# A hand-written instruction order laid out anew: a fused attention and token-mixing kernel

## The chip, the cores and the metric

The kernel runs on one core of a Trainium2 chip. The metric is the device time of one execution in microseconds; the time before is the median of three executions. A core has five engines that run side by side, each through its own list of instructions in order: TensorE (PE; its weight loads are shown as PEld), VectorE (DVE), ScalarE (ACT), GpSimd (POOL) and SyncE (SP). They wait for one another by semaphores. SP, ACT and POOL also issue DMAs, which run on 16 shared DMA engines.

## The reference

For each of 8 batches, 8 heads, 576 rows `q`, `k`, `v` of 64 and 32 packing rows `p` (all float32):

```python
p_packed = sm_attn(p, k, v)                # 32 rows attend to 576
out      = sm_attn(q, p_packed, p_packed)  # 576 rows attend to the 32 results
x = out.transpose(0, 2, 1, 3).reshape(B, S, H * D)      # [8, 576, 512]
wq, wk = x @ w_q, x @ w_k                               # [8, 576, 64] each
W_tok  = scale * einsum('bsd,btd->bst', wq, wk)
mixed  = einsum('bst,btd->bsd', W_tok, x)
result = maximum(mixed, 0) @ w_out                      # [8, 576, 512] float32
```

`sm_attn` is softmax attention with a scale of 1/8.

## The kernel before, in words

There is no scheduler. A string `ORDER` (lines 13 to 57) names every step of the program, and a loop at the end records them in that order. An engine's instruction list is the steps of that engine as the string gives them; the place of two steps of different engines in the string has no effect but through waits. A step is written `NAME.batch.part`, then `@A`, `@V` or `@P` for ScalarE, VectorE or GpSimd (nothing: TensorE for matmuls, SP for stores, GpSimd for loads), then `=` and the PSUM banks that it fills. `WARM.n=bank` is n times 128 columns of dummy matmul, recorded at L617.

The steps of one batch, in the order of its data:

| step | engine | what |
|---|---|---|
| `LD.k`, `LD.v`, `LD.q` | POOL's queue | loads, cast to bf16 on the way; `v` is two DMAs. For batches 0 and 7 `q` comes in halves: `LD.q0`, `LD.q7` are half 1, `LD.r0`, `LD.r7` half 0 |
| `KT`, `QV` (L237) | DVE | transposes of k and q; part 2 is both halves, parts 0 and 1 one half |
| `S1` (L282), `X1` (L293), `TE` (L237) | PE, ACT, DVE | first scores, their exponentials, their transpose |
| `PV` (L315), `RC`, `PP` (L319, L323), `PT` (L237) | PE, DVE | packed rows, normalised, transposed |
| `QK` (L336), `QKE`, `QD` (L128 or L132, L130) | PE, ACT or DVE, POOL | packed rows times `w_k` and `w_q`, copied out of PSUM, half of it doubled |
| `S2` (L373), `X2` (L378) | PE, ACT | second scores, exponentials |
| `HA`, `RS`, `RR`, `AM` (L388, L394, L399, L405) | POOL or DVE | row sums, reciprocals, the product with them |
| `AT` (L414, L419), `AE` | PE, ACT or DVE | transpose of the weights, copy out |
| `WKQ` (L441, L446), `WE` | PE, ACT or DVE | both projections, copy out |
| `GM` (L467), `GE`, `Y` (L477), `YE` | PE, ACT or DVE | the token mixing, contracted to a small matrix first |
| `MX` (L492), `MR` (L498), `RL`, `RLF`, `RLR` (L503, L505) | PE, ACT or DVE | mixed rows, ReLU; `MR`/`RLR` are the 64 remainder rows of a batch |
| `OT` (L540), `OE`, `OEF` | PE, ACT or DVE | output matmuls by tiles of 128 rows; part 4 is the remainder of two batches together |
| `ST`, `STF` | SP's or POOL's queue | stores of 512 KB (`ST.b.0`, `ST.b.1`: halves of a batch), 256 KB (`ST.b.4`, `STF`) |
| `OH`, `OEH`, `STH` (L578, L132, L588) | | the last tile of batch 7 in two column pieces given by `OHC` |

Buffers: four each for loaded k, v and q (`NL`), six for output rows `o` (`NO`; batch 6 reuses batch 0's, batch 7 batch 1's), two for the exponentials (`NE`). In the program every DMA of POOL's queue waits for the landing of the one eight places before it. `HOLD.v7` is a 128-byte DMA on SP that waits for `v7` to land; all of SP's stores stand behind it.

TensorE's first 35 us are three batches' first steps with `WARM` between them; from the first output matmul (`OT.0.0`) on, `OT` blocks of a batch are laid between the steps of the batches that follow.

Of the kernel before, what the change touches and what calls it, by code (L numbers as in the profile page):

```python
# [23 lines left out]
RS.1.2@V RR.1.2@V S2.1.1=2,3 X2.1.0@A RS.1.0@V RR.1.0@V WARM.1=6 PV.2.0=6,7 PV.2.1 X2.1.1@A RS.1.1@V RC.2@V  # L24
LD.v3 QD.1@P AM.1.2@P AT.1.2=4 RR.1.1@V AM.1.0@P WARM.5=5 AT.1.0=5 AM.1.1@P LD.k4 PP.2.0@V AE.1.2@A PP.2.1@V
PT.2@V QK.2=4 AE.1.0@A QKE.2@A QD.2@P QV.2.2@V LD.q3 LD.v4 AT.1.1=0 AE.1.1@A WKQ.1.0=2,3 WKQ.1.2 WKQ.1.1
WE.1.0@V S2.2.2=6,7 WE.1.1@A X2.2.2@A S2.2.3=4,5 X2.2.3@A GM.1=1 OT.0.0=2,3 GE.1@V Y.1=6,7 OT.0.1 YE.1@A
RS.2.4@V OE.0.0@A MR.1=0,1 MX.1.1=4,5 RLR.1@A RR.2.4@V OT.0.2=6,7 LD.q4 OT.0.3 KT.3.2@V AM.2.3@P OE.0.1@V
RL.1.1@A S1.3=2,3,0,1 X1.3.0@A AM.2.2@P OT.1.4=4 TE.3.0@V LD.k5 AT.2.2=5 X1.3.1@A TE.3.1@V AT.2.3=2 AE.2.3@V
LD.v5 MX.1.0=6,7 AE.2.2@V PV.3.0=0,1 PV.3.1 OEF.1.4@A WKQ.2.0=2,3 WKQ.2.1 RC.3@V PP.3.1@V RL.1.0@A WKQ.2.2  # L30
WE.2.2@A OT.1.2=4,5 OT.1.3 PP.3.0@V PT.3@V QK.3=6 OE.1.1@A LD.q5 KT.4.2@V S1.4=0,1,2,3 GM.2=7 OT.1.0=4,5
X1.4.1@A LD.k6 GE.2@A QKE.3@V X1.4.0@A QV.3.2@V TE.4.1@V Y.2=2,3 YE.2@A S2.3.2=6,7 X2.3.2@A S2.3.3=0,1
X2.3.3@A MX.2.0=2,3 TE.4.0@V RL.2.0@A MR.2=6,7 RLR.2@V OT.1.1 MX.2.1=6,7 RL.2.1@A OE.1.0@A PV.4.0=0,1 QD.3@P
PV.4.1 RS.3.4@V RR.3.4@V LD.v6 AM.3.3@P AM.3.2@P RC.4@V OT.2.0=2,3 OT.2.1 LD.q6 OE.2.0@A PP.4.0@V PP.4.1@V
PT.4@V QK.4=6 AT.3.3=7 QV.4.2@V AT.3.2=0 AE.3.2@A LD.k7 S2.4.2=4,5 AE.3.3@V X2.4.2@A S2.4.3=2,3 X2.4.3@A
KT.5.2@V WKQ.3.0=0,1 WKQ.3.1 WKQ.3.2 RS.4.4@V RR.4.4@V QKE.4@A WE.3.2@A S1.5=4,5,2,3 X1.5.1@A LD.v7 TE.5.1@V
OT.2.2=6,7 AM.4.3@P QD.4@P AM.4.2@P GM.3=0 X1.5.0@A TE.5.0@V GE.3@A OT.2.3 Y.3=2,3 YE.3@V PV.5.0=4,5 PV.5.1
HOLD.v7 MR.3=0,1 RC.5@V PP.5.1@V OE.2.1@A MX.3.0=2,3 PP.5.0@V PT.5@V MX.3.1=6,7 RLR.3@A RL.3.0@A OT.3.4=0
RL.3.1@A AT.4.2=1 AE.4.2@A OEF.3.4@A QV.5.2@V AT.4.3=5 AE.4.3@V ST.1.4@P QK.5=4 QKE.5@V QD.5@P S2.5.2=2,3
X2.5.2@A KT.6.2@V S2.5.3=6,7 X2.5.3@A HA.5@P WKQ.4.0=0,1 WKQ.4.2 LD.q7 WKQ.4.1 WE.4.2@A OT.3.0=2,3  # L40
S1.6=4,5,6,7 X1.6.0@A GM.4=0 GE.4@V TE.6.0@V LD.r7 OT.3.1 X1.6.1@A TE.6.1@V Y.4=0,1 OE.3.0@A RS.5.4@V RR.5.4@V
PV.6.0=4,5 YE.4@A PV.6.1 MX.4.0=6,7 RC.6@V RL.4.0@A PP.6.0@V AM.5.3@P PP.6.1@V PT.6@V MX.4.1=2,3 AM.5.2@P
OT.3.2=0,1 OT.3.3 RL.4.1@A QK.6=4 QKE.6@A QV.6.2@V ST.2.1 S2.6.2=6,7 X2.6.2@A S2.6.3=2,3 ST.3.4 MR.4=4,5
X2.6.3@A OE.3.1@V RLR.4@V KT.7.2@V AT.5.2=6 AE.5.2@A AT.5.3=7 OT.4.0=0,1 OT.4.1 AE.5.3@A WKQ.5.0=4,5 WKQ.5.2
OE.4.0@A ST.1.1@P WKQ.5.1 RS.6.4@V WE.5.2@A RR.6.4@V ST.4.0 ST.0.1@P S1.7=2,3,6,7 X1.7.1@A AM.6.3@V ST.3.0@P
OT.4.2=0,1 GM.5=4 TE.7.1@V OT.4.3 AT.6.3=5 X1.7.0@A TE.7.0@V GE.5@A OE.4.1@A AM.6.2@P AT.6.2=4 ST.2.0 Y.5=6,7
YE.5@A ST.0.0 ST.3.1 PV.7.0=2,3 QV.7.1@V AE.6.3@V QV.7.0@V AE.6.2@A QD.6@P PV.7.1 RC.7@V PP.7.0@V PP.7.1@V
PT.7@V MR.5=0,1 RLR.5@A MX.5.1=6,7 RL.5.1@A MX.5.0=4,5 RL.5.0@V WKQ.6.0=0,1 WKQ.6.1 WKQ.6.2 WE.6.2@A OT.5.4=2
OEF.5.4@A S2.7.1=6,7 ST.5.4 ST.1.0 GM.6=3 GE.6@V X2.7.1@A RS.7.1@V RR.7.1@V S2.7.2=0,1 X2.7.2@A S2.7.0=4,5
QK.7=2 X2.7.0@A RS.7.0@V RR.7.0@V Y.6=6,7 YE.6@A OT.5.2=0,1 MX.6.1=4,5 QKE.7@A MX.6.0=6,7 AM.7.1@P RS.7.2@V  # L50
RR.7.2@V MR.6=2,3 OT.5.3 RLR.6@V RL.6.0@V RL.6.1@A OE.5.1@A ST.4.1 AM.7.0@P OT.5.0=2,3 AM.7.2@P AT.7.0=4
AE.7.0@A AT.7.1=5 AE.7.1@V AT.7.2=6 AE.7.2@V OT.6.2=0,1 OEF.6.2@A QD.7@P WKQ.7.0=4,5 WKQ.7.2 WKQ.7.1 WE.7.0@A
WE.7.1@A STF.6.2 OT.6.0=6,7 OT.6.1 GM.7=0 OE.6.0@V OT.5.1 OE.5.0@V ST.5.1@P GE.7@A Y.7=4,5 OT.6.3 OEF.6.3@V
ST.6.0 STF.6.3 YE.7@A ST.5.0 MR.7=6,7 RLR.7@A MX.7.0=4,5 RLF.7.0.1@A RLF.7.0.0@V MX.7.1=2,3 RLF.7.1.0@A
OT.7.4=0 OEF.7.4@A ST.7.4 RLF.7.1.1@V OT.7.1=6 OEF.7.1@V OT.7.0=7 STF.7.1 OT.7.2=1 OEF.7.0@A OH.7.0=0 STF.7.0
OEF.7.2@A STF.7.2 OEH.7.0@V STH.7.0 OH.7.1=5 OEH.7.1@A STH.7.1@A
"""


# [1 line left out]
def kernel(  # L61
# [46 lines left out]
    def bank(n, shape, dt=fp32):  # L108
        if isinstance(n, list):
            assert n[1] == n[0] + 1  # L110
            ap = ps_all[:, n[0]:n[1] + 1].rearrange("a k n -> a (k n)")
# [12 lines left out]
        return ap.rearrange(f"a ({' '.join(names)}) -> a {' '.join(names)}", **dims)

    def copy(eng, o, i):
        if eng == "A":
            nc.scalar.activation(o, i, COPY)  # L128
        elif eng == "P":
            nc.gpsimd.tensor_copy(o, i)  # L130
        else:
            nc.vector.tensor_copy(o, i)  # L132
# [441 lines left out]
    def OH(b, h, eng, bk):  # L574
        n0, n1 = OHC[h]
        ps = T["oh", h] = bank(bk, [n1 - n0])
        for j in range(NJ):
            nc.tensor.matmul(ps, T["relu", b][:, j // 2, j % 2, 3 * P:4 * P], wout[:, j, n0:n1],  # L578
                             start=j == 0, stop=j == NJ - 1)
# [4 lines left out]

    def STH(b, h, eng, bk):
        q = nc.scalar if eng == "A" else nc.sync
        n0, n1 = OHC[h]
        q.dma_start(orows(b)[:, :, 3 * D + n0:3 * D + n1], T["o", b][:, 3, n0:n1])  # L588
# [62 lines left out]
```

## Time and profile before

| | |
|---|---|
| median of three executions | 104.38 us (104.2 to 105.15) |
| the profiled execution | 104.42 us, span 102.6 us from the first to the last instruction |
| busy, of the span | PE 91%, DVE 72%, ACT 63%, POOL 52% |
| granted TensorE clock | 0.993 of full speed |
| HBM | 30.15 MB read, 9.44 MB written |
| DMA rate | 203 to 234 GB/s (bytes written) while loads run, about 410 GB/s while stores run |

A profile has these views, which the next part quotes: the page (busy times, shares, the chain of work that ended last, followed back from the last instruction), a table by stretches of time (length, busy us and instruction count of PE, PEld, DVE, ACT, POOL, then granted clock, DMA share and GB/s), the timeline (start, duration, engine, line, operation, output <- input, shapes, count, and in brackets the idle time before it and what ended it), and answers for one tile (duration, start, time from a DMA's issue to its landing).

### The profile page before, as it was taken

The page shows a single profiled execution, that of the slowest core. Times are in us where ns is not written, and L with a number is a line of the kernel's source. Part 1 is how long each engine was busy: PE and PEld are TensorE (multiplying, and loading weights), DVE is VectorE, ACT ScalarE, POOL GpSimd, SP SyncE. Part 2 cuts the span into 40 slices and gives each one's busy share as a digit, 9 for nine tenths or more (in the row PEclk, how much of TensorE's full clock was granted, in tenths as well). Part 3 has the DMA queues.
Part 4 walks back from the last instruction along what each step waited for, and adds up shares of the span by engine and source line. Part 5 has one row for each costly group of instructions (what it writes and reads, how often), then busy time and mean ns, then how long its engine had stood idle before and what let it go on. Part 6 is the DMA issues. An engine that isn't in the chain of part 4 may idle for free.

```text
span 102.6 us, 3594 instructions
## 1 busy us (share of the span) xinstructions
PE 93.2 (91%) x1536; PEld 55.1 (54%) x1536; DVE 73.5 (72%) x140; ACT 65.0 (63%) x111; POOL 53.1 (52%) x83
## 2 busy tenths in 40 slices
...
GB/s 18 234 230 207 211 215 209 207 210 213 203 212 207 214 209 209 213 210 207 212 210 208 211 212 204 216 211 205 250 250 387 412 413 409 417 388 294 346 370 127
DMA packets 13567, 25.13 MB, mean 245 GB/s; under 512 B 1072, under 2 KB 6448, under 8 KB 13552
## 3 DMA queue, kind: packets, MB, share of 16 engines
...
HBM read 30.15 MB, written 9.44 MB: 386 GB/s over the span
## 4 chain that ended last, share of the span: by engine, by line
PE 64%; DVE 9%; ACT 8%; DMA 7%; POOL 4%; issue 3%; DVEq 0%; POOLq 0%; ACTq 0%
PE ps L540 26%; PE ps L617 9%; DMA k_sb<-in_k_dram 7%; PE ps L373 5%; PE ps L315 4%; ACT e1T L293 4%; POOL a L405 4%; PE ps L282 3%; PE ps L419 3%; PE ps L446 3%; PE ps L467 3%; DVE rs L394 2%; PE ps L441 2%; PE ps L336 2%; DVE kT L237 2%
## 5 line engine op out<-in xcount | busy, mean ns | idle before, releaser
L540 PE MATMUL ps<-wout,relu 128*128 128x512 bf16 x124 | 30.6, 380 | 0.0
L405 POOL TENSOR_TENSOR a<-e,rr 128x256 bf16<-128x256 f32 (+2 forms) x18 | 19.5, 1099 | 16.4 <-DVE rr L399 6.4
L617 PE MATMUL ps<-o 128*128 128x128 f32 (+3 forms) x76 | 20.0, 410 | 1.2 <-DVE o L135 1.2
L540 PEld LDWEIGHTS <-relu 128*128 128x128 bf16 x124 | 10.7, 98 | 11.7 <-issue 1.1
L128 ACT ACTIVATE o<-ps 128x1024 f32<-128x1024 f32 (+2 forms) x13 | 11.3, 870 | 5.4 <-PE ps L540 5.2
L617 PEld LDWEIGHTS ps<-o 128*128 128x128 f32 x76 | 11.8, 217 | 5.2 <-issue 3.6
L503 ACT ACTIVATE relu<-ps 128x1024 bf16<-128x1024 f32 (+1 forms) x14 | 12.9, 966 | 1.1 <-PE ps L492 1.1
L293 ACT ACTIVATE e1T<-ps 128x576 bf16<-128x576 f32 x16 | 9.8, 655 | 5.2 <-PE ps L282 4.6
L378 ACT ACTIVATE e<-ps 128x256 f32<-128x256 f32 (+2 forms) x19 | 11.2, 622 | 2.5 <-PE ps L373 2.4
L394 DVE TENSOR_REDUCE rs<-e 128x16 f32<-128x512 f32 (+2 forms) x13 | 10.9, 841 | 2.3 <-ACT e L378 2.2
L173 POOL DMA_DIRECT2D v_sb<-in_v_dram x16 | 10.0, 629 | 4.2 <-DMA v_sb<-in_v_dram 1.6
L237 DVE STREAM_TRANSPOSE kT<-k_sb 128x1152 uint32<-128x1152 uint32 (+1 forms) x9 | 11.0, 1226 | 1.4 <-DMA k_sb<-in_k_dram 1.3
L237 DVE STREAM_TRANSPOSE qT<-q_sb 128x1152 uint32<-128x1152 uint32 (+1 forms) x10 | 11.0, 1104 | 0.0
L132 DVE COPY o<-ps 128x1024 f32<-128x1024 f32 (+2 forms) x7 | 6.7, 977 | 5.2 <-PE ps L540 2.7
L237 DVE STREAM_TRANSPOSE e<-e1T 128x288 uint32<-128x288 uint32 x16 | 7.4, 468 | 3.1 <-ACT e1T L293 2.6
L128 ACT ACTIVATE aT<-ps 128x128 bf16<-128x128 f32 (+2 forms) x11 | 5.0, 464 | 5.7 <-PE ps L419 3.3
L128 ACT ACTIVATE wkq<-ps 128x448 bf16<-128x448 f32 (+1 forms) x10 | 7.2, 729 | 1.8 <-PE ps L446 1.7
L315 PE MATMUL ps<-v_sb,e 64*64 64x192 bf16 x288 | 7.5, 245 | 0.8 <-DVE e L237 0.5
L315 PEld LDWEIGHTS <-e 64*64 64x64 bf16 x288 | 5.9, 107 | 2.6 <-DVE e L237 2.0
L373 PEld LDWEIGHTS <-qT 64*128 64x128 bf16 x320 | 5.4, 94 | 2.6 <-DVE qT L237 1.5
L446 PE MATMUL ps<-aT,pqk 128*128 128x256 bf16 (+1 forms) x48 | 6.8, 246 | 0.0
L373 PE MATMUL ps<-ppT,qT 64*128 64x64 bf16 x320 | 6.6, 190 | 0.1
...
## 6 DMA issues: line engine op xcount, KB each, us to landing
...
q_sb<-in_q_dram POOLq DMA_DIRECT2D x4, 288.0 KB, 10.5
...
```

Source lines behind the costliest of these rows:

```text
L128: nc.scalar.activation(o, i, COPY)
L173: nc.gpsimd.dma_start(v_bufs[b % NL][halves(i), 0:7:2], src)
L237: nc.vector.transpose(o, i)
L293: nc.scalar.activation(e1T[:, x], T["s1", b][x].rearrange("a c m -> a m c"), EXP, scale=scale)
L315: nc.tensor.matmul(T["pv", b][halves(cc), i], lhsT, rhs, start=n == 0, stop=n == R - 1, skip_group_check=True)
L373: nc.tensor.matmul(ps[:, y, t - t0, i], lhsT, rhs, start=e == 0, stop=e == 1)
L378: nc.scalar.activation(e2[:, t0:t1].rearrange("a t (i y n) -> a y (t i) n", i=2, y=2), T["s2", b, c].rearrange("a y t i n -> a y (t i) n") ...
L394: nc.vector.tensor_reduce(rs[:, t0 * H:t1 * H], src, axis=AX, op=ADD)
L405: e.tensor_tensor(a2[:, t0:t1].rearrange("a t i (u l) -> a (t i u) l", l=L), e2v(b, c), T["rr", b][:, t0 * H:t1 * H].to_broadcast((P, (t1 ...
L503: nc.scalar.activation(o, i, RELU)
L540: nc.tensor.matmul(ps, lhsT, wout[:, j, :], start=j == 0, stop=j == NJ - 1)
L617: nc.tensor.matmul(bank(int(bk), [w]), warm[:, 0:P], rhs, start=True, stop=True)
```

## The change

The change is to `ORDER` and to `OHC` alone. Up to `LD.k1`, and through the first scores `S1.0`, nothing is moved but small preparations. Behind that the list is laid out anew in places:

- At the start, `QV.0.1` stands ahead of `PT.0` and `QV.0.0` on VectorE, where `PT.0`, `QV.0.0`, `QV.0.1` stood. `LD.q2` stands between `AM.0.2` and `AM.0.0` on GpSimd, where it followed all of `AM.0`. `LD.k2` stands later, `LD.v2` sooner. `QK.0` stands between parts of `S2.0`. `S1.1` precedes `AT.0.1` (it followed `WKQ.0`), `S1.2` precedes `Y.0`, and with them `X1.1` and `TE.1`. `AE.0.1`, `GE.0` go to VectorE, `AE.0.0`, `QKE.1` to ScalarE. The dummy matmuls are 51 units after `S1.0` where they were 43.
- Later, `LD.q7`, `LD.r7` precede `LD.v7`; `QK.5` moves from ahead of `S2.5` to ahead of `Y.4`; `AE.2.2` stands between `TE.3.1` and `TE.3.0`; some copies change between ScalarE and VectorE.
- Stores: `ST.2.0`, `ST.2.1` (both halves of batch 2) and `ST.3.4` (a remainder tile; `ST.1.4` was there already) go to POOL's queue, `ST.1.1`, `ST.3.0`, `ST.5.1` to SP's. `ST.0.1` stands last in POOL's queue. `OEF.6.2` goes from ScalarE to VectorE, ahead of `WE.7.1`, which comes there too.
- At the end, the 384-column piece of the last tile is stored by ScalarE's queue and the 128-column piece by SP's; VectorE copies both.

The diff, cut to the start, the stores and the end:

```diff
-OHC = (0, 384), (384, 512)
+OHC = (384, 512), (0, 384)
 ...
-LD.g0 LD.v0 LD.r0 LD.q0 LD.k1 NC.0@V PX.0@V NC.1@A PX.1@V SET.aff@P SET.idb@V SET.v3@P KT.0.0@V SET.mask@P
-WC.1@P WC.0@P LD.k2 SET.v1@P LD.v1 SET.v2@P KT.0.1@V WARM.4=0 WARM.22.128=0 S1.0=0,1,2,3 X1.0.1@A TE.0.1@V
-X1.0.0@A TE.0.0@V WARM.8=4 PV.0.0=4,5 PV.0.1 RC.0@V PP.0.0@V PP.0.1@V LD.q1 PT.0@V WARM.6=6 QK.0=6 QKE.0@A
-QV.0.0@V QV.0.1@V QD.0@P WARM.4=7 S2.0.2=2,3 X2.0.2@A RS.0.2@V RR.0.2@V S2.0.0=0,1 LD.v2 S2.0.1=4,5 X2.0.0@A
-RS.0.0@V RR.0.0@V X2.0.1@A RS.0.1@V RR.0.1@V AM.0.2@P WARM.6=7 AT.0.2=7 AE.0.2@A AM.0.0@P WARM.5=6 AT.0.0=6
-KT.1.2@V AM.0.1@P WARM.3=2 AT.0.1=7 AE.0.1@A AE.0.0@V WKQ.0.0=2,3 WKQ.0.2 WE.0.0@A LD.q2 WKQ.0.1 KT.2.2@V
-S1.1=0,1,4,5 WE.0.1@A GM.0=6 X1.1.0@A TE.1.0@V GE.0@A WARM.2=7 Y.0=2,3 YE.0@V S1.2=0,1,6,7 MR.0=2,3 X1.1.1@A
-TE.1.1@V MX.0.0=4,5 X1.2.0@A LD.O PV.1.0=0,1 TE.2.0@V PV.1.1 X1.2.1@A TE.2.1@V RC.1@V LD.k3 PP.1.0@V PP.1.1@V
-PT.1@V MX.0.1=6,7 QV.1.2@V RLR.0@A QK.1=2 QKE.1@V RL.0.0@A WARM.3=3 S2.1.2=4,5 S2.1.0=0,1 RL.0.1@A X2.1.2@A
+LD.g0 LD.v0 LD.r0 LD.q0 LD.k1 NC.0@V PX.0@V NC.1@A PX.1@V SET.aff@P SET.idb@V KT.0.0@V KT.0.1@V WARM.4=0
+WARM.22.128=0 S1.0=0,1,2,3 X1.0.0@A TE.0.0@V WC.0@P X1.0.1@A TE.0.1@V WARM.8=4 PV.0.0=4,5 PV.0.1 RC.0@V
+SET.mask@P PP.0.1@V PP.0.0@V QV.0.1@V PT.0@V QV.0.0@V WARM.12=6 S2.0.2=6,7 X2.0.2@A S2.0.0=0,1 X2.0.0@A
+SET.v1@P SET.v2@P WC.1@P QK.0=2 S2.0.1=4,5 LD.k2 X2.0.1@A RS.0.2@V RR.0.2@V LD.v1 LD.q1 RS.0.0@V RR.0.0@V
+LD.v2 AM.0.2@P WARM.4=3 AT.0.2=3 LD.q2 RS.0.1@V AM.0.0@P WARM.7=6 AT.0.0=6 RR.0.1@V KT.1.2@V S1.1=0,1,4,5
+AM.0.1@P AT.0.1=7 QKE.0@A AE.0.1@V AE.0.2@A AE.0.0@A KT.2.2@V X1.1.0@A TE.1.0@V QD.0@P WKQ.0.0=2,3 WKQ.0.2
+X1.1.1@A TE.1.1@V WE.0.0@A WKQ.0.1 WE.0.1@A WARM.3=6 GM.0=6 S1.2=0,1,4,5 LD.O X1.2.1@A GE.0@V Y.0=2,3 YE.0@V
+LD.k3 PV.1.0=6,7 PV.1.1 TE.2.1@V X1.2.0@A MX.0.0=4,5 RL.0.0@A MR.0=2,3 RLR.0@A TE.2.0@V SET.v3@P LD.v3
+MX.0.1=0,1 RL.0.1@A RC.1@V PP.1.0@V PP.1.1@V PT.1@V QV.1.2@V WARM.2=6 QK.1=6 QKE.1@A QD.1@P WARM.7=7
+S2.1.2=4,5 X2.1.2@A RS.1.2@V S2.1.0=2,3 RR.1.2@V AM.1.2@P X2.1.0@A S2.1.1=0,1 WARM.4=7 PV.2.0=6,7 PV.2.1
 ...
```

The two DMA queues from `LD.q6` on, as the lists give them:

```
POOL before: LD.q6 LD.k7 LD.v7 AM.4.3 QD.4 AM.4.2 ST.1.4 QD.5 HA.5 LD.q7 LD.r7 AM.5.3 AM.5.2
             ST.1.1 ST.0.1 ST.3.0 AM.6.2 QD.6 AM.7.1 AM.7.0 AM.7.2 QD.7 ST.5.1
POOL after:  LD.q6 LD.k7 AM.4.2 AM.4.3 LD.q7 LD.r7 LD.v7 ST.1.4 HA.5 ST.2.0 AM.5.2 AM.5.3
             ST.2.1 ST.3.4 QD.5 AM.6.2 QD.6 ST.0.1 AM.7.1 QD.7 AM.7.0 AM.7.2
SP before:   HOLD.v7 ST.2.1 ST.3.4 ST.4.0 ST.2.0 ST.0.0 ST.3.1 ST.5.4 ST.1.0 ST.4.1 STF.6.2
             ST.6.0 STF.6.3 ST.5.0 ST.7.4 STF.7.1 STF.7.0 STF.7.2 STH.7.0
SP after:    HOLD.v7 ST.3.0 ST.4.0 ST.1.0 ST.1.1 ST.5.4 ST.0.0 ST.5.1 STF.6.2 ST.4.1 ST.3.1
             ST.6.0 ST.5.0 STF.6.3 ST.7.4 STF.7.2 STF.7.1 STF.7.0 STH.7.0
```

More of the change, by code (lines that the diff above doesn't have):

```diff
@@ L23 @@
-PT.1@V MX.0.1=6,7 QV.1.2@V RLR.0@A QK.1=2 QKE.1@V RL.0.0@A WARM.3=3 S2.1.2=4,5 S2.1.0=0,1 RL.0.1@A X2.1.2@A
[L24 to L56, printed above, removed]
+LD.g0 LD.v0 LD.r0 LD.q0 LD.k1 NC.0@V PX.0@V NC.1@A PX.1@V SET.aff@P SET.idb@V KT.0.0@V KT.0.1@V WARM.4=0
+WARM.22.128=0 S1.0=0,1,2,3 X1.0.0@A TE.0.0@V WC.0@P X1.0.1@A TE.0.1@V WARM.8=4 PV.0.0=4,5 PV.0.1 RC.0@V
@@ new lines @@
+LD.k3 PV.1.0=6,7 PV.1.1 TE.2.1@V X1.2.0@A MX.0.0=4,5 RL.0.0@A MR.0=2,3 RLR.0@A TE.2.0@V SET.v3@P LD.v3
+MX.0.1=0,1 RL.0.1@A RC.1@V PP.1.0@V PP.1.1@V PT.1@V QV.1.2@V WARM.2=6 QK.1=6 QKE.1@A QD.1@P WARM.7=7
+S2.1.2=4,5 X2.1.2@A RS.1.2@V S2.1.0=2,3 RR.1.2@V AM.1.2@P X2.1.0@A S2.1.1=0,1 WARM.4=7 PV.2.0=6,7 PV.2.1
+RS.1.0@V RR.1.0@V AM.1.0@P X2.1.1@A RS.1.1@V RC.2@V RR.1.1@V AM.1.1@P AT.1.2=4 PP.2.0@V PP.2.1@V AE.1.2@A
+WARM.4=5 AT.1.0=5 AE.1.0@A PT.2@V QK.2=2 QKE.2@A AT.1.1=3 AE.1.1@A QV.2.2@V WKQ.1.0=0,1 WKQ.1.2 WE.1.0@V
```

30 lines of the change are left out of this document (added).

## The prediction

> **What bounds the kernel now.** I read the page first, then a table of busy times by stage, then the timeline. From the page, the span, TensorE's row, the chain that ended last, and the bytes:
>
> ```profile
> span 102.6 us, 3594 instructions
> PE 93.2 (91%) x1536; PEld 55.1 (54%) x1536; DVE 73.5 (72%) x140; ACT 65.0 (63%) x111; POOL 53.1 (52%) x83
> PE 64%; DVE 9%; ACT 8%; DMA 7%; POOL 4%; issue 3%; DVEq 0%; POOLq 0%; ACTq 0%
> HBM read 30.15 MB, written 9.44 MB: 386 GB/s over the span
> ```
>
> The chain is TensorE's for two thirds. The busy share hides that much of the early work is WARM, dummy matmuls, so I ask stage by stage how long TensorE sat idle once the output matmuls have begun (first number: length; second: PE busy; last: DMA rate):
>
> ```profile
> 36.00:54.00 18.00, 17.77 (x295) 8.83 (x293) 15.03 (x26) 13.63 (x21) 9.44 (x12) 1.00 1.15 210
> 54.00:58.00 4.00, 3.23 (x102) 2.43 (x101) 3.43 (x4) 3.38 (x6) 3.01 (x5) 1.00 1.18 210
> 58.00:66.00 8.00, 7.95 (x180) 4.87 (x177) 6.63 (x13) 7.39 (x13) 4.92 (x7) 1.00 1.15 212
> 66.00:70.00 4.00, 3.52 (x93) 1.76 (x62) 3.05 (x9) 2.99 (x5) 2.45 (x4) 1.00 1.10 208
> 70.00:98.50 28.50, 28.41 (x395) 16.06 (x393) 21.91 (x36) 21.27 (x38) 9.07 (x12) 1.00 1.01 348
> ```
>
> Idle from 36 to 98.5 is 0.23 + 0.77 + 0.05 + 0.48 + 0.09 = 1.62 us in 62.5. From 36 on the kernel is a queue of matmuls with no room: the change leaves their number as it is, so whatever start it gives this queue is carried to the end, less what it saves of 1.62. Before 36 nothing is full. There it is a chain of latencies, and WARM only fills. So the start decides, and I walk it step by step.
>
> **The change, batch 0.** In the timeline before (PP, PT, QV, S2, AM, LD.q2, AT, AE, WE, GM follow one another; the last two lines are the load LD.q0 alone, issued at 4.3):
>
> ```profile
> 14.16 0.31 DVE L237 STREAM_TRANSPOSE ppT<-pp 128x128 uint32<-128x128 uint32 x1
> 14.39 1.40 DVE L237 STREAM_TRANSPOSE qT<-q_sb 128x576 uint32<-128x576 uint32 x2
> 15.96 0.78 PE L373 MATMUL ps<-ppT,qT 64*128 64x64 bf16 x40
> 17.53 0.62 POOL L405 TENSOR_TENSOR a<-e,rr 128x256 bf16<-128x256 f32 x1 [0.34 <-DVE rr L399]
> 18.36 2.06 POOL L405 TENSOR_TENSOR a<-e,rr 128x512 bf16<-128x512 f32 x2 [0.21 <-DVE rr L399]
> 20.36 0.76 POOL L182 DMA_DIRECT2D q_sb<-in_q_dram  x1
> 20.47 0.40 PE L419 MATMUL ps<-idb,a 128*128 128x128 bf16 x4
> 20.90 0.60 ACT L128 ACTIVATE aT<-ps 128x512 bf16<-128x512 bf16 x1 [2.16 <-PE ps L419]
> 22.10 0.54 ACT L128 ACTIVATE wkq<-ps 128x448 bf16<-128x448 f32 x1 [0.17 <-PE ps L446]
> 22.41 0.62 PE L467 MATMUL ps<-wkq,a 128*128 128x64 bf16 x10
> L179 POOL DMA_DIRECT2D q_sb<-in_q_dram x1: 581/581/581, 4.3 to 4.3; - x1
> DMA to landing us min/median/max: 10.5/10.5/10.5
> ```
>
> (1) Before, VectorE ran PT.0, then QV.0.0 (it needs LD.r0), then QV.0.1 (it needs LD.q0). After, QV.0.1 stands first, ahead of PT.0 and QV.0.0. Its half of q lands at 4.3 + 10.5 = 14.8; VectorE is free at 14.16 and stands. Behind it are PT.0 (0.31) and QV.0.0 (0.70), and S2.0 needs all three. S2.0.2 starts at 14.8 + 0.70 + 0.31 + 0.70 and the 0.17 that lay between QV's end (15.79) and S2 (15.96): 16.7, +0.7. The longer WARM.12 ahead of it on TensorE only fills. Bounds: 0, if q0 landed by 14.16, and +0.8.
>
> (2) LD.q2 now stands between AM.0.2 and AM.0.0 on GpSimd. AM.0.2 runs 18.25 to 18.85, LD.q2 takes 0.76, and the two others 2.06: AM.0.1 ends at 21.65 instead of 20.42, +1.2. The loads and memsets moved about on GpSimd ahead of that (LD.k2 and LD.v1 later, LD.v2 sooner) are issued while k1 is still in flight, so the DMA does not run dry: nothing. Were that cover gone, the empty stretch would be added to every later landing.
>
> (3) S1.1 now precedes AT.0.1, and X1.1.0 and X1.1.1 precede WE.0.0 and WE.0.1 on ScalarE. AM.0.0 ends at 20.6, AT.0.0 0.45 after, AE.0.0 (0.60) at 21.7; two X1 (1.19 by the row below) and two WE (0.54 each) put WE.0.1's end at 23.65 to 24.0 against 22.64. GM.0 ends 0.39 later (22.41 + 0.62 − 22.64), at 24.05 to 24.4 against 23.03.
>
> **Batch 1.** Of before: KT.2, GE.0, TE.1.0, YE.0, both X1.2, PT.1, QV.1, QK.1 and S2.1; last, from the chain, WARM.5.
>
> ```profile
> 20.97 1.38 DVE L237 STREAM_TRANSPOSE kT<-k_sb 128x1152 uint32<-128x1152 uint32 x1 [0.38 <-DMA k_sb<-in_k_dram]
> 23.19 0.27 ACT L128 ACTIVATE g<-ps 128x128 bf16<-128x128 f32 x1
> 23.32 0.48 DVE L237 STREAM_TRANSPOSE e<-e1T 128x288 uint32<-128x288 uint32 x1 [0.98 <-ACT e1T L293]
> 23.81 0.42 DVE L486 TENSOR_SCALAR y<-ps 128x256 bf16<-128x256 f32 x1
> 24.28 1.19 ACT L293 ACTIVATE e1T<-ps 128x576 bf16<-128x576 f32 x2 [0.28 <-PE ps L282]
> 26.84 0.31 DVE L237 STREAM_TRANSPOSE ppT<-pp 128x128 uint32<-128x128 uint32 x1
> 27.08 1.34 DVE L237 STREAM_TRANSPOSE qT<-q_sb 128x1152 uint32<-128x1152 uint32 x1
> 27.21 0.41 PE L336 MATMUL ps<-wqk,ppT 64*64 64x128 bf16 x8 [0.96 <-DVE ppT L237]
> 28.47 0.78 PE L373 MATMUL ps<-ppT,qT 64*128 64x64 bf16 x40
> 18.43 1.16 PE ps L617 x4
> ```
>
> (4) VectorE's order is AE.0.1, KT.2, TE.1.0, TE.1.1, GE.0, YE.0, TE.2.1, TE.2.0, RC.1, PP.1, PT.1. AE.0.1 ends at about 22.5; KT.2 (1.38) 23.9; two TE (0.48 each) 24.7; GE.0, which moved here from ScalarE, 25.0; Y.0 (0.35 lay between GE.0's end and YE.0's start) and YE.0 (0.42) 25.7; two TE 26.55. The last TE before ended at 24.28 + 1.19 + 0.51 = 25.98 and PT.1 started 0.86 after; 26.55 + 0.86 is 27.4, +0.55. The early S1.1 and S1.2 have won half of the 1.2 back.
>
> (5) Then TensorE: QK.1, and WARM.7 where WARM.3 stood, then S2.1.2. QK.1 starts at 27.21 + 0.55 = 27.75 and takes 0.34 until the next; WARM.5 took 1.16, so WARM.7 takes 1.5 to 1.6. S2.1.2 starts at 29.6. QV.1 has been done since 27.65 + 1.34 = 29.0, so the filler itself is the gate. Against 28.47 that is +1.1. Bounds: +0.5 (QV.1 the gate) and +1.4.
>
> (6) From S2.1.2 to OT.0.0 both orders hold the same chain (X2, RS, RR, AM.1 three times, AT, AE, WKQ, S2.2, GM.1); WARM.4 and PV.2 fit in before RC.2 is due. Taken: +1.05 at OT.0.0.
>
> **The long stage.** Blocks of output matmuls stand between the steps as before. Two waits of before, AT.3.3's and PV.6's:
>
> ```profile
> 54.46 0.62 PE L419 MATMUL ps<-idb,a 128*128 128x128 bf16 x8 [0.45 <-POOL a L405]
> 68.14 0.94 PE L315 MATMUL ps<-v_sb,e 64*64 64x192 bf16 x36 [0.47 <-DVE e L237]
> ```
>
> AE.2.2 now stands between TE.3.1 and TE.3.0, so PV.3 starts 0.15 later; AT.3.3's wait, which ends with AM.3.3, absorbs most. QK.5 moves from ahead of S2.5 (leaving about 0.3 until QV.5, now ahead of PT.5, is done) into the idle before PV.6 (0.47): even. ST.2.0, ST.2.1 and ST.3.4 on GpSimd cost it 0.6 each, and three stores leave it; behind them wait AM.5, QD.5 and AM.6.2, each some us early: nothing, and 0.6 for each were they late. Sum +0.05, bounds −1.62 (all idle gone) and +0.5.
>
> **The end.** HOLD.v7, VectorE's and ScalarE's last copies, ScalarE's store, a store stage's rate, and OEF.6.2 for below:
>
> ```profile
> 75.34 0.62 SPq L572 DMA_DIRECT2D touch<-v_sb  x1
> 98.40 0.56 DVE L132 COPY o<-ps 128x384 f32<-128x384 f32 x1 [1.69 <-PE ps L578]
> 98.57 0.28 ACT L128 ACTIVATE o<-ps 128x128 f32<-128x128 f32 x1 [0.28 <-PE ps L578]
> 98.88 0.65 ACTq L588 DMA_DIRECT2D out_dram<-o  x1
> 84.00:86.00 2.00, 2.00 (x16) 0.82 (x15) 1.76 (x7) 1.50 (x4) 1.47 (x2) 1.00 1.03 413
> 88.60 0.60 ACT L128 ACTIVATE o<-ps 128x512 f32<-128x512 f32 x1 [0.55 <-PE ps L540]
> ```
>
> Both last copies are VectorE's now: 98.40 + 0.56 + about 0.3 = 99.25 for the second where ScalarE had it at 98.85. Some is won since the wide store leaves at 98.97 by ScalarE. Taken +0.15, bounds +0.1 and +0.4. With v7 loaded last, HOLD.v7 lets SP's stores go after 0.59 MB more, 0.59 / 0.21 = 2.8 us later, at 78.1; 9.44 MB at 413 GB/s end at 101.0, before an end moved past 103, so this is hidden. PV.7 finds v7 landed.
>
> **Sum.** 1.05 + 0.05 + 0.15 = 1.25. The profiled execution took 104.42 (span 102.6 and 1.8 around it): 105.67. It lies 0.04 above the median of 104.38, so I forecast 105.6; with the steps' bounds 105.1 to 106.2.
>
> **Rivals.** (a) *The start loses only the filler.* If q0 lands by 14.2, steps 1 to 4 shrink to nothing at PT.1 and WARM.7 alone costs 0.5: 104.4 + 0.5 + 0.2 = 105.1. For it: landing times move by some tenths. Against: it needs 0.6. (b) *Not slower: the long stage pays back.* The other engines get S1.1 and S1.2 sooner, and if the re-laid order closes TensorE's idle, up to 1.62 returns: 104.4 + 1.25 − 1.6 = 104.0. It decides where idle after OT.0.0 falls below 0.4. For it: 0.47 and 0.45 are single waits, each beside a moved step. Against: AT.3.3's chain (RS, RR, AM.3) is unchanged. (c) *A store gates the end.* ST.0.1 now stands last in GpSimd's queue, and OEF.6.2, on VectorE ahead of WE.7.1 and so GM.7, overwrites what it stores. From v7's landing at 78.1, the queue has 2.1 MB to the end of ST.0.1: at the whole 413 GB/s until 83.2, at half until 88.3, at 0.4 of it until 90.8. OEF.6.2 is due at 88.60 + 1.1 = 89.7. In the last case VectorE stands 1.1 us: 106.7.
>
> [...]
>
> **How the numbers follow.** Forecast 0.57, (a) 0.16, (b) 0.17, (c) 0.10. One per cent (1.04 us, about what a measurement of this kernel can tell from no change) lies at 103.3 and 105.4. Faster: a third of (b), where steps 1 and 5 fail too: 0.06. Slower: 0.50 of the forecast and (c): 0.60. Within: 0.34. The range reaches into (b) and (c): 104.4 to 106.6.
>
> **What would show it.** Right: VectorE idle until 14.8 ahead of a 128x576 qT; S2.0 at 16.7; AM.0.1's end at 21.6; S2.1 at 29.6 straight behind a dummy matmul; OT.0.0 1.05 later; idle after it near 1.6. Wrong: S2.1 before 29.0, idle after OT.0.0 under 0.8, a VectorE wait for out_dram near 90, or an end of matmuls before 99.

## The result and the profile after

The changed kernel takes 107.18 us (median of five, 107.03 to 107.35) against 104.38: ratio 1.025, 95% interval 1.0224 to 1.0276. It is slower by 2.8 us where 1.25 were forecast. The profiled execution took 107.22 us, span 105.4. From its page: span, TensorE's row, the chain that ended last.

```profile
span 105.4 us, 3571 instructions
PE 93.7 (89%) x1519; PEld 55.3 (52%) x1534; DVE 71.0 (67%) x139; ACT 66.1 (63%) x112; POOL 53.2 (50%) x83
PE 47%; DVE 18%; DMA 10%; ACT 8%; POOL 6%; issue 6%; DVEq 0%; ACTq 0%; POOLq 0%
```

TensorE does the same work, but for eight more units of filler, in a longer span, and the chain runs through other engines for longer. (The list holds one dummy instruction fewer, which is two matmul records; 15 of the 1534 are missing here, so TensorE's idle time can't be summed as it was before.) The lost time has four places. The first is the start, in the timeline of VectorE and TensorE:

```profile
14.80 0.78 DVE L237 STREAM_TRANSPOSE qT<-q_sb 128x576 uint32<-128x576 uint32 x1 [0.62 <-DMA q_sb<-in_q_dram]
16.49 0.53 PE L373 MATMUL ps<-ppT,qT 64*128 64x64 bf16 x24 [0.52 <-DVE qT L237]
26.92 0.31 DVE L237 STREAM_TRANSPOSE ppT<-pp 128x128 uint32<-128x128 uint32 x1
27.17 1.38 DVE L237 STREAM_TRANSPOSE qT<-q_sb 128x1152 uint32<-128x1152 uint32 x1
27.65 1.77 PE L617 MATMUL ps<-o 128*128 128x512 f32 x4
29.36 0.78 PE L373 MATMUL ps<-ppT,qT 64*128 64x64 bf16 x40
```

`QV.0.1` waits for q0 at the front and S2.0 starts 0.53 late. By `PT.1` (26.92, before 26.84) that is nearly made up. Then the seven units of filler take 1.77 us, and S2.1 starts at 29.36, straight behind them, 0.89 later than before; QV.1 was done at 28.55.

The second place is VectorE's `RR.2.4`, in the timeline of the kernel before:

```profile
36.45 1.49 DVE L394 TENSOR_REDUCE rs<-e 128x40 f32<-128x1280 f32 x1 [0.43 <-ACT e L378]
38.03 0.40 DVE L399 RECIPROCAL rr<-rs 128x40 f32<-128x40 f32 x1
```

and of the kernel after:

```profile
37.32 1.49 DVE L394 TENSOR_REDUCE rs<-e 128x40 f32<-128x1280 f32 x1 [0.37 <-ACT e L378]
39.31 0.40 DVE L399 RECIPROCAL rr<-rs 128x40 f32<-128x40 f32 x1 [0.51 <-DVE rs L394]
```

VectorE idles 0.51 us ahead of it, behind its own row sums, which ended at 38.81; before, it followed them by 0.10. The third place is TensorE's `PV.6`, in the timeline of the kernel after:

```profile
69.26 0.61 PE L315 MATMUL ps<-v_sb,e 64*64 64x192 bf16 x20
70.41 0.53 PE L315 MATMUL ps<-v_sb,e 64*64 64x192 bf16 x16 [0.54 <-issue]
```

TensorE stands for 0.54 us between the 20th and the 21st matmul of one `PV` step. "issue" in the bracket says that nothing in the profile released it.

The fourth place is the stores. The table by stages (last column GB/s), of the kernel before:

```profile
88.00:90.00 2.00, 2.00 (x23) 1.30 (x22) 0.38 (x2) 1.45 (x4) 0.35 (x1) 1.00 1.03 415
90.00:92.00 2.00, 2.00 (x19) 0.98 (x17) 0.88 (x1) 0.35 (x2) 0.00 (x0) 1.00 1.01 410
```

and of the kernel after:

```profile
84.00:86.00 2.00, 2.00 (x49) 1.39 (x50) 1.63 (x4) 1.96 (x6) 0.00 (x0) 1.00 1.03 406
88.00:90.00 2.00, 2.00 (x17) 1.13 (x15) 0.59 (x2) 1.99 (x3) 1.18 (x2) 1.00 0.48 184
90.00:92.00 2.00, 1.95 (x26) 1.34 (x26) 1.48 (x3) 0.82 (x2) 0.00 (x0) 1.00 0.43 174
...
102.00:104.00 2.00, 0.00 (x0) 0.00 (x0) 0.00 (x0) 0.00 (x0) 0.00 (x0) 1.00 0.60 212
```

SyncE's queue in the timeline of the kernel after; a row of two issues spans from the start of the first to the end of the second:

```profile
85.64 4.91 SPq L561 DMA_DIRECT2D out_dram<-o  x2
91.20 0.54 SPq L592 DMA_DIRECT2D out_dram<-o  x1
91.79 1.25 SPq L561 DMA_DIRECT2D out_dram<-o  x2
```

The answer for the line that stores the two pieces of the last tile, after:

```profile
DMA to landing us min/median/max: 3.4/3.4/3.5
```

and before:

```profile
DMA to landing us min/median/max: 2.5/2.6/2.8
```

SyncE issues `ST.0.0` at 85.64, then stands until `OE.5.1` has written what `ST.5.1` stores (90.02), then until `OEF.6.2` (91.20). Behind these two in its queue are `ST.4.1` and `ST.3.1`, 1 MB whose data were there by 81.3 us. They are issued at 91.79 and 92.44. The DMA engines ran below half of 400 GB/s for four microseconds; what they did not move then is in the way at the end, and the last store takes 3.45 us to land.

### The profile page after: what moved, and what is told of

It reads as the page before. It is cut to its first block, busy times and chain, and to the rows that moved or that the text cites. A ratio compares the mean times of both kernels' runs of the same rounds, so it can differ in the third digit from the quotient of the medians.

```text
span 105.4 us, 3571 instructions
## 1 busy us (share of the span) xinstructions
PE 93.7 (89%) x1519; PEld 55.3 (52%) x1534; DVE 71.0 (67%) x139; ACT 66.1 (63%) x112; POOL 53.2 (50%) x83
## 4 chain that ended last, share of the span: by engine, by line
PE 47%; DVE 18%; DMA 10%; ACT 8%; POOL 6%; issue 6%; DVEq 0%; ACTq 0%; POOLq 0%
PE ps L540 19%; DMA q_sb<-in_q_dram 10%; PE ps L315 4%; PE ps L617 4%; ACT e L378 4%; DVE kT L237 4%; POOL a L405 4%; PE ps L373 4%; DVE rs L394 3%; DVE e L237 3%; PE ps L419 3%; DVE qT L237 3%; PE ps L446 2%; PE ps L282 2%; PE ps L492 2%
## 5 line engine op out<-in xcount | busy, mean ns | idle before, releaser
L540 PE MATMUL ps<-wout,relu 128*128 128x512 bf16 x112 | 29.4, 380 | 0.9 <-issue 0.3
L617 PE MATMUL ps<-o 128*128 128x128 f32 (+3 forms) x74 | 21.5, 440 | 1.7 <-DVE o L135 1.2
L503 ACT ACTIVATE relu<-ps 128x1024 bf16<-128x1024 f32 (+1 forms) x15 | 14.0, 965 | 1.2 <-PE ps L492 0.9
L128 ACT ACTIVATE o<-ps 128x1024 f32<-128x1024 f32 (+1 forms) x12 | 11.5, 956 | 4.9 <-PE ps L540 4.7
L132 DVE COPY o<-ps 128x1024 f32<-128x1024 f32 (+3 forms) x8 | 6.5, 824 | 4.9 <-PE ps L540 2.1
L128 ACT ACTIVATE wkq<-ps 128x896 bf16<-128x896 f32 (+1 forms) x9 | 6.7, 758 | 1.9 <-PE ps L446 1.5
```

Source lines behind the costliest of these rows:

```text
L503: nc.scalar.activation(o, i, RELU)
L540: nc.tensor.matmul(ps, lhsT, wout[:, j, :], start=j == 0, stop=j == NJ - 1)
L617: nc.tensor.matmul(bank(int(bk), [w]), warm[:, 0:P], rhs, start=True, stop=True)
```

## The experiments

The traces allow one table for all runs. From the third column on, each is a distance between steps within one execution, in us, so that an early or late landing of the first loads (q0 between 14.2 and 15.4 us) does not blur it. A distance runs from the start of the first step to the start of the second; "last ReLU" is the end of `RLF.7.1.1`, "landing" the last landing of a store. The last column compares with the kernel before as it ran beside that kernel. There it took 103.98 to 104.20 us, not 104.38, so against the times that the expectations name, a measured time is lower by some 0.2 to 0.4 us; the ratios are not touched by this.

| kernel | S2.0 starts | S2.0 to S2.1 | S2.1 to S1.3 | S1.6 to MX.4.0 | last ReLU to landing | ratio to before |
|---|---|---|---|---|---|---|
| before | 15.96 | 12.50 | 11.45 | 3.27 | 6.31 | 1 |
| after | 16.49 | 12.87 | 11.65 | 4.02 | 7.33 | 1.025 (1.0224 to 1.0276) |
| a_fill3 | 16.43 | 12.06 | 11.69 | 4.02 | 7.17 | 1.0188 (1.0151 to 1.0224) |
| b_fill7 | 15.46 | 13.30 | 11.43 | 3.26 | 6.11 | 1.0069 (1.0044 to 1.0094) |
| a_qv | 16.07 | 12.86 | 11.67 | 3.92 | 7.18 | 1.0231 (1.0194 to 1.0267) |
| a_store | 16.27 | 12.87 | 11.67 | 4.25 | 6.25 | 1.0164 (1.0125 to 1.0203) |
| a_qke5 | 16.03 | 12.86 | 11.68 | 3.98 | 7.27 | 1.0275 (1.0237 to 1.0313) |
| a_shift | 15.99 | 12.87 | 11.67 | 3.33 | 7.01 | 1.0155 (1.0121 to 1.0188) |
| a_p12 | 16.23 | 12.87 | 11.66 | 3.33 | 7.35 | 1.0198 (1.0160 to 1.0236) |
| a_p24 | 17.07 | 12.87 | 11.66 | 3.34 | 6.92 | 1.0263 (1.0229 to 1.0297) |
| a_dve | 16.05 | 12.87 | 11.36 | 4.26 | 7.27 | 1.0233 (1.0193 to 1.0274) |
| a_fs | 16.22 | 12.15 | 11.68 | 3.33 | 6.27 | 1.0024 (1.0007 to 1.0041) |
| a_all | 15.52 | 12.56 | 11.36 | 3.33 | 6.53 | 1.0004 (0.9988 to 1.0021) |
| a_tail | 15.59 | 12.77 | 11.37 | 3.34 | 6.16 | 0.9993 (0.9981 to 1.0005) |

The two stretches left out, S1.3 to S1.6 (25.8 us) and MX.4.0 to the last ReLU (26.3 to 26.5), are the same in all of them to 0.2 us. After less before, column by column: 0.53 + 0.37 + 0.20 + 0.75 + 1.02 = 2.87, and the last store landed 2.84 us later.

**The filler behind QK.1.** a_fill3 takes the change's filler back, b_fill7 puts it alone into the old order.

```diff
 a_fill3, in the kernel after
-QK.1=6 QKE.1@A QD.1@P WARM.7=7
+QK.1=6 QKE.1@A QD.1@P WARM.3=7
 b_fill7, in the kernel before
-WARM.3=3 S2.1.2=4,5
+WARM.7=3 S2.1.2=4,5
```

> The kernel after, with three units of dummy matmul behind QK.1 where it has seven (one word of the order). Theory F (the filler is the gate of S2.1 and its delay is carried to the end): S2.1 starts when QV.1 is done, near 28.6 us, where the kernel after has 29.36; the first output matmul comes about 0.75 earlier, and the whole takes 106.4 to 106.6 against 107.2. Rival A (the queue behind has other gates, a VectorE step near 39 us or a stall of TensorE near 70): S2.1 is earlier but half or more of it is gone by 70 us, and the time is 107.0 or more.

> The kernel before, with seven units of filler behind QK.1 instead of three: the one word of the change that the runs so far hold for its largest cost at the start, put alone into the old order. Theory F: S2.1 starts 0.75 to 0.9 us later, all of it is carried to the end, ratio 1.007 to 1.009. Rival P (the old order has slack of its own, 0.47 us at PV.6 and 0.45 at AT.3.3): half of it or more is taken up, ratio 1.004 or less.

In a_fill3, TensorE's timeline:

```profile
27.60 0.91 PE L617 MATMUL ps<-o 128*128 128x384 f32 x2
28.49 0.77 PE L373 MATMUL ps<-ppT,qT 64*128 64x64 bf16 x40
```

S2.1 starts at 28.49, as QV.1 allows (its end: 28.44). S2.0 to S2.1 falls by 0.81, and rises by 0.80 in b_fill7, with 0.69% of the time (0.72 us): the old order has no slack that takes it up. So theory F holds both ways. In a_fill3 the time fell by 0.6%, 0.65 us.

The same column shows what the new layout of batch 1 is worth: with equal filler it needs 12.06 where the old one needs 12.50. It gains 0.44, and the filler spends 0.81. (S2.1 itself, at 28.49, is no earlier than the 28.47 of before: S2.0 starts 0.47 later.)

**The order of VectorE at the start.**

```diff
-QV.0.1@V PT.0@V QV.0.0@V
+PT.0@V QV.0.0@V QV.0.1@V
```

> The kernel after, with VectorE's order PT.0, QV.0.0, QV.0.1 as the kernel before has it, instead of QV.0.1 first. It asks whether the wait for q0 at the front, the first step of the prediction, costs anything at the end. Theory Q (S2.1 follows PT.1 through QK.1 and the filler, and PT.1 follows this chain): S2.0 starts 0.3 to 0.5 us earlier, PT.1 and S2.1 as much, and the ratio to the kernel before falls from 1.025 to 1.021 or 1.022. Rival K (the slack of batch 1 takes it up): S2.0 is earlier, PT.1 is not, and the ratio stays 1.024 to 1.027.

By the time, inconclusive. S2.0 came 0.42 earlier, S2.1 and PT.1 with it, but in this execution q0 had landed at 14.19, before VectorE was free (PT.0 starts at 14.38), so the new order would not have waited either. The ratio lies between the two expectations, and its interval reaches into both. What the traces show speaks for theory Q. In all nine kernels with the new order at the start, S2.0 starts 1.71 or 1.72 us after q0 lands, and in all of them with seven units behind QK.1 S2.1 follows 12.86 or 12.87 later, whether S2.0 starts at 15.99 or at 17.07. In a_p24 q0 landed at 15.36, VectorE waited 1.59 us in front of `QV.0.1`, and S2.0 and S2.1 were both 0.58 later than in the kernel after.

That q0 was so late in a_p24 may come of that run's own edit, finer filler at the start (shown further down). In the other 13 traces q0 lands 1.35 to 1.41 us after r0, there 2.37. The first 16 KB packet of the instruction queue starts at 15.25 to 16.29 us in the others, behind q0; with 24 records of filler more ahead it started at 13.28, between r0 and q0, and took 0.89 us. That it held up q0 fits and is not shown.

**The order of the stores.**

```diff
-ST.1.1 ... ST.5.4 ST.0.0 ST.5.1 STF.6.2 ST.4.1 ST.3.1 ST.6.0
+ST.1.1 ... ST.0.0 ST.4.1 ST.3.1 ST.5.4 ST.5.1 STF.6.2 ST.6.0
```

(SyncE's list; the program's other lists are the same.)

> The kernel after, with ST.0.0, ST.4.1 and ST.3.1 (1.5 MB whose data are ready before 82 us) moved in SyncE's queue to ahead of ST.5.4, whose data come at 85.2. Nothing is computed in another order. Theory S (SyncE's queue stood for late data from 88 to 92 us, the DMA rate fell to 180 GB/s there, and the bytes not moved then are moved after the last store is issued): no window between 83 and 100 us under 350 GB/s except where nothing is left to store, the last store lands 2.5 us after its issue instead of 3.45, and the whole takes 106.1 to 106.5 against 107.2. Rival L (the last pieces take their time from the way the last tile is cut and from their queues, not from the backlog): the dip goes but the last store still takes 3.3 us or more, and the time is 107.1 or more.

The stages of a_store, and its answer for the last tile's stores:

```profile
88.00:90.00 2.00, 2.00 (x17) 1.13 (x15) 0.56 (x2) 2.00 (x3) 1.21 (x2) 1.00 1.01 399
90.00:92.00 2.00, 1.95 (x25) 1.32 (x25) 1.51 (x3) 0.84 (x3) 0.00 (x0) 1.00 0.95 371
92.00:94.00 2.00, 2.00 (x22) 0.97 (x21) 0.63 (x1) 0.66 (x2) 0.00 (x0) 1.00 0.72 278
94.00:96.00 2.00, 2.00 (x15) 0.72 (x14) 1.27 (x3) 1.52 (x3) 0.00 (x0) 1.00 0.14 56
```

```profile
DMA to landing us min/median/max: 2.4/2.4/2.4
```

Theory S holds. The low windows are now from 92 to 96, where SyncE has issued everything computed by then, so nothing is left behind for the end; the last pieces land 2.4 us after their issue, and last ReLU to landing falls by 1.08. The ratio falls by 0.9%.

**TensorE's pause inside PV.6.** Two rivals: a step of another engine, or TensorE's own instructions.

```diff
 a_qke5: QKE.5 ahead of OE.3.0 on ScalarE
-OE.3.0@A ... YE.4@A ... QKE.5@A
+QKE.5@A OE.3.0@A ... YE.4@A
 a_shift: the same filler ahead of S2.0, in pieces of 128 columns
-WARM.12=6
+WARM.12.128=6
 a_p12: the same with the filler ahead of AT.0.2
-WARM.4=3
+WARM.4.128=3
 a_p24: the same with the filler ahead of PV.0
-WARM.8=4
+WARM.8.128=4
```

> The kernel after, with QKE.5 on ScalarE ahead of OE.3.0 instead of behind YE.4, so that it ends near 69.2 us instead of 70.40. It is the other half of the question what holds TensorE inside PV.6. Rival D (PV.6 waits for QKE.5): the stall of 0.54 us is gone and the time falls by about 0.5, to 106.7. Theory I (TensorE stands for its own instructions): the stall stays at the same place with about 0.5 us, and the time is 107.1 to 107.3.

> The kernel after, with the twelve units of dummy matmul ahead of S2.0 in pieces of 128 columns instead of 512: the same columns, but 36 more matmul and weight-load records stand ahead of everything behind. It asks what holds TensorE for 0.54 us inside PV.6 near 70 us, where the profile names no semaphore. Theory I (TensorE stands for its own instructions, which come in blocks of 16 KB): the stall leaves this place, since the block's boundary now falls 36 records earlier; it is gone or stands at another instruction, and the time is between 106.6 and 107.2. Rival D (a step of another engine holds it, such as QKE.5, which ends at 70.40): the stall stays between the two parts of PV.6 with 0.5 us, and the time is 107.2.

> The kernel after, with the four units of filler ahead of AT.0.2 in pieces of 128 columns: 12 records of matmuls and weight loads more ahead of PV.6, where a_shift has 36 more. In the runs so far TensorE's pause near 70 us has always stood at the same record (number 2229 of its matmuls and weight loads in the trace), and with 36 more records it was gone. Theory I (TensorE runs out of its own instructions at a fixed record): the pause, if there is one, stands 12 records or 6 matmuls earlier, so between the 14th and 15th matmul of PV.6 instead of the 20th and 21st. A pause that stays behind the 20th matmul is against it. Its length: 0.3 to 0.8 us, or nothing if 12 records are enough for the block to come in time. Time: 105.7 to 107.2.

> The same question with 24 records more, from the eight units of filler ahead of PV.0 in pieces of 128 columns. Theory I: a pause, if there is one, behind the 8th matmul of PV.6; it is gone if the block now comes in time, as with 36. Time: 105.7 to 107.2. A pause that stays behind the 20th matmul is against it.

The timeline of a_qke5, ScalarE's `QKE.5` and TensorE's `PV.6`:

```profile
68.73 0.38 ACT L128 ACTIVATE pqk<-ps 128x256 bf16<-128x256 f32 x1 [0.48 <-PE ps L336]
68.81 0.61 PE L315 MATMUL ps<-v_sb,e 64*64 64x192 bf16 x20
69.92 0.53 PE L315 MATMUL ps<-v_sb,e 64*64 64x192 bf16 x16 [0.50 <-issue]
```

`PV.6` in a_fill3:

```profile
68.43 0.68 PE L315 MATMUL ps<-v_sb,e 64*64 64x192 bf16 x22
69.59 0.52 PE L315 MATMUL ps<-v_sb,e 64*64 64x192 bf16 x14 [0.47 <-issue]
```

in a_shift:

```profile
68.76 0.94 PE L315 MATMUL ps<-v_sb,e 64*64 64x192 bf16 x36
```

and in a_p12:

```profile
69.04 0.94 PE L315 MATMUL ps<-v_sb,e 64*64 64x192 bf16 x36
```

With `QKE.5` done at 69.11 the pause is still there at 69.42: rival D falls. In a_fill3 the filler is one instruction shorter, which is four records of matmuls and weight loads, or two matmuls of `PV.6`; the pause has moved behind by just these two, from the 20th to the 22nd. Counted in the traces, it stands at the same record, number 2229, in all six kernels that have it at that point (after, a_fill3, a_store, a_qke5, a_qv, a_dve), whatever instruction that is. With 12, 24 or 36 records more ahead of it, it is gone, though the steps keep their order; that it is gone, and not moved by as many records, is one of the two outcomes that theory I had named. So in these runs it hangs on how many instructions TensorE has had, and moving the one step that was suspected on another engine left it in place. It costs 0.69 us of the stretch S1.6 to MX.4.0 (4.02 against 3.33), up to 0.93 in other kernels. The times follow for a_p12 (1.0198) and a_shift (1.0155, below the range expected; its S2.0 is 0.50 earlier and its end 0.32 shorter besides); in a_p24 the late q0 hides it.

That the pause is the loading of instructions is the author's reading. The profile's page of the kernel after has a queue of kind instruction (packets, MB, share):

```profile
q8 instruction: 12, 0.20, 0.7%
```

and its view of the DMA queues between 67.5 and 70.5 us:

```profile
q0 software_dynamic: 287, 0.62, 109.8%
q8 instruction: 1, 0.02, 2.0%
```

That is 12 packets of 16 KB, one of them just here, while the loads keep the DMA engines busy. The kernel before, which has no pause, has a packet near this place too. But the traces hold the start of each packet, and that tells the kernels apart. For the eighth packet, in us:

| kernel | start of S1.6 to start of packet | start of packet to first matmul of PV.6 | pause | start of packet to first matmul behind the pause |
|---|---|---|---|---|
| after | 1.19 | 1.22 | 0.54 | 2.37 |
| a_fill3 | 1.37 | 1.04 | 0.47 | 2.20 |
| a_qv | 1.09 | 1.32 | 0.45 | 2.37 |
| a_store | 1.32 | 1.09 | 0.77 | 2.47 |
| a_qke5 | 1.08 | 1.33 | 0.50 | 2.44 |
| a_dve | 1.35 | 1.06 | 0.78 | 2.45 |
| the other eight | -0.79 to 0.10 | 2.31 to 3.20 | none | |

In the six kernels with the pause the packet starts about 1 us or more later against the work, and TensorE goes on 2.20 to 2.47 us after the packet's start in all six, however long it stood. In the eight others PV.6 begins 2.31 us or more after the packet's start.

So the late packet goes with the pause in every trace, but no run held a packet back by itself: that TensorE stood for the instructions in it is the author's reading and not shown, and what makes this packet late in this layout stays open.

**VectorE's pause at RR.2.4.**

```diff
-SET.aT2@V SET.idf@V
+SET.aT2@V SET.idf@V SET.aT0@V SET.aT1@V SET.aT2@V
```

> The kernel after, with the pads of the three aT buffers cleared a second time on VectorE in its first idle microseconds: six short instructions more ahead of everything on that engine. In the kernel after and in the four kernels run so far, RR.2.4 on VectorE starts 0.44 to 0.48 us after its semaphore instruction has ended, where the kernel before has 0.04, and S1.3 on TensorE then waits 0.22. Theory V (VectorE stands there for its own instructions, as TensorE did inside PV.6): the pause leaves RR.2.4, S1.3 comes 0.2 us earlier against S2.1, and the time falls by 0.1 to 0.2, ratio 1.023 to 1.025. Rival W (something in the layout holds RR.2.4): the pause stays at RR.2.4 with 0.4 us and the ratio stays 1.025 to 1.027.

VectorE in a_dve:

```profile
36.89 1.49 DVE L394 TENSOR_REDUCE rs<-e 128x40 f32<-128x1280 f32 x1 [0.36 <-ACT e L378]
38.48 0.40 DVE L399 RECIPROCAL rr<-rs 128x40 f32<-128x40 f32 x1
```

The pause is gone with six short instructions more ahead of it: 38.38 to 38.48 is the 0.10 of the kernel before, and S2.1 to S1.3 falls by 0.3. It stood at the same record in all nine kernels of the new layout without them, and it is gone in a_all and a_tail, which have them. So here too more instructions ahead, six of them, removed the pause of 0.44 to 0.48 us, and theory V holds so far. That it is the loading of instructions is not shown. In a_dve, a_all and a_tail a packet of 8 KB, of a second instruction queue, starts at 28.3 to 28.8 us where the others have it after 41 us, so with the six ahead that packet came earlier; but in the kernel after no packet of that queue starts within 3 us of the pause. Nor is the count alone the cause: in the kernel before `RR.2.4` is VectorE's 58th instruction too, semaphores not counted, and has no pause. The time hardly fell (1.0233, an interval that 1.025 lies in), as TensorE arrived at its own pause sooner and stood 0.78 us there in place of 0.54.

**All together.** a_fs is a_fill3, a_store and a_shift in one; a_all has besides the edits of a_qv and a_dve; a_tail has the old end besides.

```diff
 a_tail, in a_all
-OHC = (384, 512), (0, 384)
+OHC = (0, 384), (384, 512)
-OT.7.2 OT.7.1 OT.7.0 OH.7.1 OH.7.0   (their copies and stores go with them)
+OT.7.1 OT.7.0 OT.7.2 OH.7.0 OH.7.1
```

> The kernel after with three edits of the runs before together: three units of filler behind QK.1, the filler ahead of S2.0 in pieces of 128 columns, and ST.0.0, ST.4.1, ST.3.1 ahead of ST.5.4. It asks whether the three costs add up. If they do (0.75 for the filler, 0.75 for the pause inside PV.6, 1.0 for the backlog of stores): 2.5 us less than the kernel after, ratio 1.001 to 1.005. If they hide one another, the ratio stays above 1.010.

> The three edits of a_fs and besides VectorE's old order PT.0, QV.0.0, QV.0.1 and its six short instructions more. If both of these give what their theories say (0.35 and 0.2), ratio 0.996 to 1.000 to the kernel before: what is left of the change then costs nothing. If not, it equals a_fs, 1.001 to 1.005.

> a_all with the end of the kernel before: the last tile in pieces of 384 and 128 columns in that order, both copied and stored as there. From the end of the last ReLU to the issue of the last store the kernel before took 3.62 us, the kernel after 3.88 and a_all 3.88. Theory E (the new end costs this difference): 3.6 us here and 0.2 to 0.3 us off the time, ratio 0.996 to 0.999, which would be a version as good as or better than both. Rival B (the last landing follows the bytes, not the issue): the last store is issued sooner and lands 2.7 to 2.9 us later, and the ratio stays 0.999 to 1.002.

The costs nearly add up: 0.6, 0.9 and 1.0% taken one by one (the last with the earlier S2.0 of a_shift in it), 2.3% together. What is left of the change in a_fs costs 0.24%. a_all is equal to the kernel before within its interval, just above what was expected (1.0004, not 0.996 to 1.000), and its start shows why no more came:

```profile
26.65 1.38 DVE L237 STREAM_TRANSPOSE qT<-q_sb 128x1152 uint32<-128x1152 uint32 x1 [0.39 <-DMA q_sb<-in_q_dram]
```

PT.1 is done at 26.26, but `QV.1` now waits for q1 to land. The start has met the loads: S2.1 came at 28.09 here and at 28.36 in a_tail, where q1 landed 0.27 later. In a_tail the last store is issued 3.68 us after the last ReLU instead of 3.88, and lands 2.48 us later, so theory E holds for that stretch; the time, 0.9993, can't be told from the kernel before, nor from a_all. No version here is faster than the kernel before by more than the measurement shows.

## Why the prediction was wrong

The direction was right, the size less than half. By its own steps:

- **Step 1** (S2.0 at 16.7 by the wait for q0): 16.49, with VectorE idle until 14.80. Right. **Step 2** (`AM.0.1` ends at 21.65): 21.44. **Step 3** (`GM.0` ends at 24.05 to 24.4): 23.96, just below. Right in their mechanism.
- **Step 4** (PT.1 at 27.4): 26.92. The step added up VectorE's queue with each duration of before; the two `TE.1` took 0.80 instead of 0.96, the last two 0.87, the copy `GE.0` started 0.4 sooner than reckoned. Batch 1 gives back 0.95 of the 1.03 us by which `AM.0.1` is late, not half.
- **Step 5** (the filler is the gate, S2.1 at 29.6): 29.36, and right in its mechanism. The filler took 1.77 us (1.71 until S2.1 starts), more than the 1.5 to 1.6 taken, on a PT.1 that came 0.48 sooner: two errors that partly cancel, so the near hit is part luck. **Step 6** (OT.0.0 1.05 later): 0.88, and carried.
- **The long stage** (+0.05, at most +0.5): +0.95 from S2.1 to the last ReLU, 66.89 to 67.83. This term failed. What it weighed was right: the stores on GpSimd, `QK.5`, `AE.2.2` and the exchanged engines cost nothing that the table shows. What it lacked was 0.20 at `RR.2.4` and 0.75 at `PV.6`, two pauses for which no semaphore and no step of the change stands. `PV.6`'s old wait for VectorE did shrink, from 0.47 to 0.07; the pause came behind it. The upper bound had been made of costs of steps alone. What shows in place of the term is that TensorE's pause goes with a packet of the instruction queue that starts about 1 us or more later against the work (1.08 to 1.37 us after the start of S1.6, against -0.79 to 0.10 where there is no pause); why that packet was late, and what the pause at `RR.2.4` is, stays open.
- **The end** (+0.15, "so this is hidden"): +1.02. This term failed. The copies cost 0.26 as bounded, and `HOLD.v7` went at 78.21, as reckoned (78.1). The stores were then reckoned as bytes at 413 GB/s, and that rate was not kept: SyncE's queue stood twice, with 1 MB of ready data behind the store that was late, and from 88 to 92 us the rate was 184 and 174 GB/s; in a_store, with ready data ahead, it was 399 and 371 there. The list of SyncE's queue and the times of `OE.5.1` and `OEF.6.2` were both in the profile of before.
- **Rival (c)** (`ST.0.1` holds `OEF.6.2`): it did not come. `ST.0.1` landed at 87.55, and `OEF.6.2` ran at 90.48 behind its matmuls. The prediction's 88.3, from half of the rate for GpSimd's queue (q0) beside SyncE's (q1), came close by luck. Between the issue of `ST.0.1` and its landing, 80.25 to 87.55, the queues moved (packets, MB, share):

```profile
q1 hardware_dynamic: 702, 2.29, 80.1%
q0 software_dynamic: 171, 0.60, 20.9%
```

That is a fifth, and no run here shows the half; it was enough because GpSimd's queue had moved 0.68 MB between 78.2 and 80.2, before SyncE's first store got going. **Rival (b)** (the long stage pays back) fell. **Rival (a)** names what set S2.1 in fact, the filler alone, at a cost of 0.8 rather than 0.5; its condition, a q0 that lands by 14.2, did not come (14.78).

Of the signs that were named as wrong, the idle time after OT.0.0 can't be read for the missing records; none of the others appeared. There was none for the DMA rate in the stage of the stores, which is where a third of the loss shows at a glance.
